# DRAINs on GpSimd's queue in the conditional blocks, and a tile's output products in one run with the next tile's score products

## The chip, the cores and the metric

One core of one Trainium2 chip runs the kernel. The metric is the device time of one execution in microseconds (us). Before the change three timed runs gave 1208.03, 1209.3 and 1210.64 us; their median, 1209.3 us, is what the change is measured against.

## What is computed

Three layers follow each other: attention inside chunks of 64 positions, a dense layer with three input matrices and a maximum between them, and a layer of eight experts of which each token takes one.

```python
scores = scale * np.matmul(q_c, k_c.transpose(0, 1, 2, 4, 3))     # 8 x 8 heads, chunks of 64 x 64
attn = softmax(scores); out = np.matmul(attn, v_c)
...
h = np.maximum(np.maximum(x @ w1, x @ w2), x @ w3)                # 4608 x 512 by 512 x 768
x = h @ w_out                                                     # 768 x 512
...
e_idx = np.argmax(x @ w_gate, axis=1)                             # one expert of 8 a token
h = np.maximum(x[mask] @ w1[e], 0.0)                              # 512 x 1024
ye = h @ w2[e]                                                    # 1024 x 512
out[mask] = gate_w[mask, None] * eom[mask, e, None] * ye
```

All is fp32; the wide products are made of three passes over split operands (`mm3`, lines 101 to 104).

## The kernel before

**Attention, 36 tiles.** A tile `a` is 128 positions of all eight heads. `att_S` (line 422) makes the scores: 16 products of 64 x 64, which TensorE does as quarters of its array, into the two banks of the PSUM tile `ps_a2` (the tiles 1 and 2 have other banks). VectorE takes the maxima (line 440), ScalarE the exponentials with their sums in eight ACTIVATEs (459), VectorE the reciprocals (465, 466), GpSimd the product with them (469). `att_P` (474) turns the result with four full transposes (485), and ScalarE copies it out (491). `att_V` (493) makes the outputs, again 16 quarter products (507), into `ps_a2` as well; ScalarE rounds them into `xth` (514) and VectorE makes the rest `xtl` (99). `quarters` (403) gives both the same first half of either bank: `[:, :, 0:HP * 64]`, that is 256 of 512 columns.

**Dense layer, nine blocks of four tiles.** `moe_f` (598) runs 18 groups of 12 matmuls of 128x512 per block (lines 102 to 104); ScalarE and VectorE bring them out over one buffer `hs` (611, 613), ScalarE and GpSimd split the result (615, 99). `moe_y` (618) and `gate` (637) follow.

**What sets the order.** In these two layers every step is recorded with an engine, an estimated duration, a priority and the keys that it reads and writes (`add`, 256); `order` (290) then plays the steps through and writes each engine's queue. So the order of each engine's instructions is fixed when the program is built, and TensorE has attention steps of the next block's tiles between the wide matmuls of the present block. A key that is read by two engines can be given an order of its own: line 271 does that for `psg` and for the tuples `("tr", ..)` and `("mm", ..)`. The key of `ps_a2` is the plain string `"a2"`, whose first character is `"a"`; the test `x[0] in ("a2", ..)` doesn't meet it.

`attention` (1051) calls the steps of a tile. From tile 7 (`2 * NA - 1`) to the last, the scores of tile `i + 1` are recorded after the outputs of tile `i` (the table `after`).

**Experts.** Tokens are gathered in blocks of 256 by expert. `step` (1149) does one block: GpSimd copies the places of block `b + 2` and gathers it (`gather_ahead`, 1133: a COPY and two indirect DMAs, lines 838 and 831), TensorE makes the two products, ScalarE scales the result (884), and GpSimd writes it with two indirect DMAs (887). 18 blocks (0 to 17) are written out straight; the rest, 18 to 25, are nested conditionals (`tail`, 1189), entered as long as the number of blocks is larger than `b`. This input has 21 blocks, so 18, 19 and 20 run. Code outside `order` runs in the order in which it is written. At the program's end each engine does a DRAIN, and a barrier follows; these and the preamble have the lines 1232 and 1212.

Of the kernel before, what the change touches and what calls it, by code (L numbers as in the profile page):

```python
# [21 lines left out]
def tile_chunk_attention_moe_moe(  # L22
# [25 lines left out]
    NTILE = NT // P  # L48
# [8 lines left out]
    NB0 = NT // BP  # L57
# [113 lines left out]
    HP = H // 2  # L171
# [88 lines left out]
    def add(eng, dur, prio, rd, wr, fn, lat=0.0, lead=0.0):  # L260
        o = Op()
        o.eng, o.dur, o.fn, o.prio, o.n = eng, dur, fn, prio, len(ops)
        o.lat, o.lead, o.at = lat, lead, None
        if eng == "PE" and lead == 0.0 and prio > 0:
            o.lead = LEAD
        need = set()
        rd, wr = list(flat(rd)), list(flat(wr))
        for x in rd:
            if x in writer:
                need.add(writer[x])  # L270
            if x == "psg" or x[0] in ("a2", "tr", "mm"):

                need.update(r for r in readers.get(x, ()) if r.eng != eng)
        for x in wr:
            if x in writer:
                need.add(writer[x])
            need.update(readers.get(x, ()))
        for x in rd:
            readers.setdefault(x, []).append(o)
        for x in wr:  # L280
            writer[x] = o
            readers[x] = []
        o.need, o.rd, o.wr = need, rd, wr
        ops.append(o)
# [115 lines left out]
        i = a % NE2  # L400
        return es[i], [("e", i), ("mx", i), ("sm", i)], mxs[i], sms[i]

    def quarters(a):


        sp = lambda x, n: x.rearrange("p (b x) -> p b x", b=n)[:, :, 0:HP * 64].rearrange("p b (a i) -> p b a i", a=HP)
        if a % 3 and a < NW:
            bk = [(ps_mm[0], ("mm", 0)), (ps_mm[1], ("mm", 1))] if a % 3 == 1 else [(ps_mm[2], ("mm", 2)), (ps_g, "psg")]
            return [(sp(x, 1), [kx], slice(i, i + 1)) for i, (x, kx) in enumerate(bk)]
        return [(sp(ps_a2, 2), ["a2"], slice(0, 2))]  # L410
# [7 lines left out]
    def att_Q(a, pr):  # L418
        for w in range(2):
            load(a, w, pr - LA)  # L420

    def att_S(a, pr):
        e, (ek, mk, sk), mx, sm = e_of(a)

        t = qk_buf[a % 3]
        parts = quarters(a)
        bank = [ps[:, i] for ps, _, hs in parts for i in range(hs.stop - hs.start)]

        def mm():
            for hp in range(HP):  # L430
                for h2 in range(2):
                    for c in range(2):
                        x = t[h64(h2), :, hp, h64(c)]
                        PE.matmul(bank[h2 if a < NAT else h2 ^ c][h64(c), hp], x[:, 0], x[:, 1], start=True, stop=True)

        add("PE", T_Q, pr + 1, [("qk", a % 3, 0), ("qk", a % 3, 1)], [x for _, kk, _ in parts for x in kk], mm)
        m2 = mx.rearrange("p (b a) -> p b a", b=2)
        for n, (ps, pk, hs) in enumerate(parts):
            add("DVE", t_dve(512 // len(parts)), pr + 1, pk, [(mk, n)],
                lambda ps=ps, hs=hs: DVE.tensor_reduce(out=m2[:, hs], in_=ps, axis=AX.X, op=ALU.max))  # L440
        ex = e.rearrange("p (a b) j -> p b a j", b=2)
        ek2, sk2 = [(ek, 0), (ek, 1)], [(sk, 0), (sk, 1)]
        if a in SUBD:
            for n, (ps, pk, hs) in enumerate(parts):
                add("DVE", t_dve(512 // len(parts)), pr + 1, pk + [(mk, n)], ek2 if len(parts) == 1 else [(ek, n)],
                    lambda ps=ps, hs=hs: DVE.tensor_tensor(
                        out=ex[:, hs], in0=ps, in1=m2[:, hs].unsqueeze(3).to_broadcast([P, hs.stop - hs.start, HP, 64]),
                        op=ALU.subtract))
            add("ACT", t_act(512), pr + 1, ek2, ek2, lambda: ACT.activation(out=e, in_=e, func=ACTF.Exp, scale=scale))
            add("DVE", t_dve(512), pr + 1, ek2, sk2, lambda: DVE.tensor_reduce(out=sm, in_=e, axis=AX.X, op=ALU.add))  # L450
        else:
            add("DVE", 0.08, pr + 1, [(mk, n) for n in range(len(parts))], [mk] + [(mk, n) for n in range(len(parts))],
                lambda: DVE.tensor_scalar(out=mx, in0=mx, scalar1=-scale, scalar2=None, op0=ALU.mult))  # L453
            for b in range(2):
                ps, pk, hs = parts[b % len(parts)]

                def fn(b=b):
                    for hp in range(HP):
                        ACT.activation(  # L459
                            out=ex[:, b, hp], in_=bank[b][:, hp], func=ACTF.Exp, scale=scale,  # L460
                            bias=mx[:, HP * b + hp:HP * b + hp + 1], accum_out=sm[:, 2 * hp + b:2 * hp + b + 1])

                add("ACT", 4 * 0.29, pr + 1, pk + [mk], [(ek, b), (sk, b)], fn)
        add("DVE", 0.08, pr + 1, sk2, sk2,
            lambda: DVE.tensor_scalar(out=sm, in0=sm, scalar1=1e-9, scalar2=None, op0=ALU.add))
        add("DVE", 0.12, pr + 1, sk2, sk2, lambda: DVE.reciprocal(out=sm, in_=sm))
        on = "DVE" if a < MULD else "POOL"
        add(on, t_dve(512) if on == "DVE" else 1.0, pr + 1, ek2 + sk2, ek2,
            lambda: (DVE if on == "DVE" else POOL).tensor_tensor(
                out=e, in0=e, in1=sm.unsqueeze(2).to_broadcast([P, H, 64]), op=ALU.mult))  # L470

    def att_P(a, pr):
        e, (ek, _, _), _, _ = e_of(a)
# [16 lines left out]
        add("PE", 0.9 if a < NAT else 0.45, pr + 2, [(ek, 0), (ek, 1)], [("tr", a % 2)], fn)  # L490
        add("ACT", t_act(512), pr + 2, [("tr", a % 2)], [("pTF", a % 2)], lambda: ACT.copy(pTF[a % 2], pp))

    def att_V(a, pr):
        j, t_ = tile_block[a]
        dst = lambda hl: xt[j % 2][hl][:, :, t_ * P:(t_ + 1) * P]
        xk = lambda hl: [("xt", j % 2, t_, hl, h2) for h2 in range(2)]
        vv, x = v_buf[a % NV], pTF[a % 2]
        bank = [ps[:, i] for ps, _, cs in quarters(a) for i in range(cs.stop - cs.start)]

        def mm():  # L500
            for hp in range(HP):
                for s in range(2):
                    for c in range(2):
                        if a < NAT:
                            PE.matmul(bank[c][h64(s), hp], vv[h64(c), hp, s], x[h64(c), hp, s], start=True, stop=True)
                        else:
                            PE.matmul(bank[c][h64(s ^ c), hp], vv[h64(s), hp, c], x[h64(s), hp, c], start=True, stop=True)

        add("PE", T_Q, pr + 3, [("v", a % NV), ("pTF", a % 2)], [x for _, kk, _ in quarters(a) for x in kk], mm)
        o = lambda hl: dst(hl).rearrange("p a (b i) -> p b a i", b=2)  # L510
        for ps, pk, cs in quarters(a):
            n = 256 * (cs.stop - cs.start)
            kx = lambda hl: [("xt", j % 2, t_, hl, i) for i in range(cs.start, 2)] if n == 256 else xk(hl)
            add("ACT", t_act(n), pr + 3, pk, kx(0), lambda ps=ps, cs=cs: ACT.copy(o(0)[:, cs], ps))
            add("DVE", t_dve(n), pr + 3, pk + kx(0), kx(1), lambda ps=ps, cs=cs: sub(DVE, o(1)[:, cs], ps, f(o(0)[:, cs])))
# [535 lines left out]
    def attention(a, n):  # L1051

        def prio(i):
            j, t = tile_block[i]
            return -100 + PS * i if j == 0 else A1 + AS1 * t if j == 1 else v0(j - 1) + AO + AS * t

        pr = [prio(i) for i in range(NTILE)]

        def score(i):
            if i < NTILE:  # L1060
                att_Q(i, pr[i])
                att_S(i, pr[i])


        before = {i: [i + 2] for i in (*range(NA - 2), NA, NA + 1)}
        after = {i: [i + 1] for i in range(2 * NA - 1, NTILE)}
        after[NA - 1] = [NA, NA + 1]
        if a == 0:
            score(0)
            score(1)  # L1070
        for i in range(a, a + n):
            att_P(i, pr[i])
            for x in before.get(i, ()):
                score(x)
            att_V(i, pr[i])
            for x in after.get(i, ()):
                score(x)

# [70 lines left out]
    def step(b):  # L1149
        scalars(b)  # L1150
        gather_ahead(b + 2)
        for c in range(4):
            for i in range(2):
                l1_mm(b, c, i)
            l1_hi(c)
            l1_lo(c)
            if c == 2:
                switch(b, (0,))
        x_T(b + 1)
        switch(b, (1,))  # L1160
        if b + 1 < NBLK:
            full[b + 1] = sval([ET.PE], 7, b + 1, 1)
        l2(b, 0)
        with tc.If(full[b] > 0):
            l2(b, 1)
        y(b, 1)
        switch(b, (2, 3))
# [69 lines left out]
```

## Time and profile before

| | |
|---|---|
| median of 3 timed runs | 1209.3 us |
| profiled execution | 1207.82 us |
| its span, first to last instruction | 1206.0 us |
| TensorE busy | 1181.2 us (98%), 9219 matmuls |
| VectorE, ScalarE, GpSimd busy | 436.7 (36%), 418.1 (35%), 195.7 (16%) us |
| TensorE's mean granted clock | 0.995 |

The profile is one execution. PE is TensorE with its matmuls, PEld its weight loads, DVE VectorE, ACT ScalarE, POOL GpSimd, SP SyncE; a q behind a name is the engine's queue (its sequencer), whose waits, branches and DRAINs aren't counted as busy. A matmul's row has its start and a modelled end, so distances between starts are what is read here. An idle time in brackets stands before the instruction, with what ended it.

### The profile page before, as it was taken

What the parts mean: (1) busy time and instruction counts of PE and PEld (TensorE: products, weight loads), DVE (VectorE), ACT (ScalarE), POOL (GpSimd) and SP (SyncE); (2) the same over time, 40 slices, a digit from 0 to 9 for tenths busy, and PEclk for the clock granted to TensorE, in tenths of its full rate; (3) what the DMA queues carried; (4) which work ended last, traced back from release to release, by engine and by line L of the source; (5) the groups of instructions that cost most, each with busy time, mean ns of one, the idle gap of its engine ahead of it and who ended that gap; (6) DMA issues with size and microseconds to landing.
All of it is one profiled execution on the core that took longest, in us unless ns stands there. A gap on an engine that the chain in (4) does not pass through costs nothing. (4 is left out here: it accounts for less than half of the span.)

```text
span 1206.0 us, 23510 instructions
## 1 busy us (share of the span) xinstructions
PE 1181.2 (98%) x9219; PEld 1035.3 (86%) x9219; DVE 436.7 (36%) x1095; ACT 418.1 (35%) x1192; POOL 195.7 (16%) x243
## 2 busy tenths in 40 slices
PE   7999999999999999999999999999999999999995
PEld 6879788897888988988879898989989989999994
DVE  7995413232232322322323452211266211511270
ACT  5575323333243332333322322212256212512271
POOL 1000111111211111111111112112112212112120
PEclk9999999999999999999999999999999999999998
DMA  8842212121121121211230015111156211511151
GB/s 283 245 140 71 86 30 87 47 58 59 35 80 53 47 69 36 80 54 35 73 106 36 1 45 201 54 45 53 46 207 241 100 44 48 180 45 62 38 171 29
DMA packets 84318, 103.06 MB, mean 85 GB/s; under 512 B 40287, under 2 KB 49503, under 8 KB 84192
## 3 DMA queue, kind: packets, MB, share of 16 engines
q1 hardware_dynamic: 77152, 79.82, 20.7%
q0 software_dynamic: 7040, 21.60, 5.6%
q8 instruction: 75, 1.23, 0.4%
q14 instruction: 51, 0.42, 0.1%
HBM read 149.55 MB, written 20.52 MB: 141 GB/s over the span
## 5 line engine op out<-in xcount | busy, mean ns | idle before, releaser
L102 PE MATMUL mm<-xth,wpc 128*128 128x512 f32 x576 | 233.8, 406 | 0.0
L104 PE MATMUL mm<-xth,wpc 128*128 128x512 f32 x576 | 226.5, 393 | 0.0
L103 PE MATMUL mm<-xtl,wpc 128*128 128x512 f32 x576 | 226.0, 392 | 0.1
L613 DVE TENSOR_TENSOR hs<-mm,hs 128x512 f32<-128x512 f32 x108 | 74.4, 688 | 184.0 <-PE mm L104 184.0
L871 DVE SCALAR_TENSOR_TENSOR wo<-mm,wo 128x512 fp32r<-128x512 f32 x64 | 43.5, 689 | 239.1 <-ACT wo L867 208.6
L104 PEld LDWEIGHTS mm<-xth,wpc 128*128 128x128 f32 x576 | 108.3, 188 | 24.7
L102 PEld LDWEIGHTS mm<-xth,wpc 128*128 128x128 f32 x576 | 108.2, 188 | 23.8
L103 PEld LDWEIGHTS mm<-xtl,wpc 128*128 128x128 f32 x576 | 108.5, 188 | 21.3 <-DVE xtl L99 0.4
L102 PE MATMUL mm<-wo,ht 128*128 128x256 f32 (+1 forms) x432 | 126.2, 292 | 0.0
L104 PE MATMUL mm<-wo,ht 128*128 128x256 f32 (+1 forms) x432 | 122.7, 284 | 0.0
L103 PE MATMUL mm<-wo,ht 128*128 128x256 f32 (+1 forms) x432 | 122.6, 284 | 0.0
L102 PE MATMUL tr<-wpc,wo 128*128 128x512 f32 x304 | 120.3, 396 | 0.0
L104 PE MATMUL tr<-wpc,wo 128*128 128x512 f32 x304 | 118.5, 390 | 0.0
L103 PE MATMUL tr<-wpc,wo 128*128 128x512 f32 x304 | 118.3, 389 | 0.0
L99 POOL TENSOR_TENSOR ht<-hs,ht 128x512 fp32r<-128x512 f32 x48 | 62.0, 1291 | 293.2 <-ACT ht L615 293.2
L887 POOL DMA_INDIRECT out_dram<-yo,S x42 | 43.7, 1042 | 355.2 <-ACT yo L884 271.4
L615 ACT CAST ht<-hs 128x512 fp32r<-128x512 f32 x54 | 33.6, 623 | 160.9 <-DVE hs L613 160.8
L459 ACT ACTIVATE rg<-a,mx 128x64 f32<-128x64 f32 x264 | 78.7, 324 | 22.1 <-DVE mx L453 22.1
L99 DVE TENSOR_TENSOR wpc<-raw,wpc 128x512 fp32r<-128x512 f32 x112 | 70.2, 684 | 39.8 <-ACT wpc L825 39.8
L102 PEld LDWEIGHTS mm<-wo,ht 128*128 128x128 f32 x432 | 81.2, 188 | 1.8 <-issue 0.4
L103 PEld LDWEIGHTS mm<-wo,ht 128*128 128x128 f32 x432 | 81.5, 189 | 0.4
L104 PEld LDWEIGHTS mm<-wo,ht 128*128 128x128 f32 x432 | 81.3, 188 | 0.0
(243 smaller groups left out, 2258.3 us busy)
## 6 DMA issues: line engine op xcount, KB each, us to landing
raw<-in_moe_w_dram SPq DMA_DIRECT2D x92, 1024.0 KB
x_scratch<-U SPq DMA_DIRECT2D x36, 258.0 KB
rg<-in_q_dram SPq DMA_DIRECT2D x36, 256.0 KB
rg<-in_k_dram SPq DMA_DIRECT2D x36, 256.0 KB
wst<-in_moe_w_dram SPq DMA_DIRECT2D x18, 512.0 KB
rg<-in_v_dram SPq DMA_DIRECT2D x128, 64.0 KB
U<-in_moe_w_out_dram SPq DMA_DIRECT2D x6, 512.0 KB
rg<-in_v_dram SPq DMA_DIRECT2D x4, 256.0 KB
```

Of the source, the lines that this page charges most:

```text
L99: eng.tensor_tensor(out=o, in0=a, in1=b, op=ALU.subtract)
L102: PE.matmul(o, ah, bh, start=first, stop=False)
L103: PE.matmul(o, ah, bl, start=False, stop=False)
L104: PE.matmul(o, al, bh, start=False, stop=last)
L459: ACT.activation(out=ex[:, b, hp], in_=bank[b][:, hp], func=ACTF.Exp, scale=scale, bias=mx[:, HP * b + hp:HP * b + hp + 1], accum_out=sm[: ...
L613: add("DVE", t_dve(N), up, [pk, hk], [hk], lambda: DVE.tensor_tensor(out=h, in0=ps, in1=h, op=ALU.max))
L615: add("ACT", t_act(N), up, [hk], [("ht", g, 0)], lambda: ACT.copy(ht[g][:, 0, :N], h))
L871: DVE.scalar_tensor_tensor(out=hT()[:, 1, fs], in0=l1_ps(c), scalar=0.0, in1=f(hT()[:, 0, fs]), op0=ALU.max, op1=ALU.subtract)
L887: POOL.indirect_dma_start(out=out, out_offset=bass.IndirectOffsetOnAxis(ap=ic[b % 4]()[:, t, 1:2].bitcast(U32), axis=0), in_=yo(b, t), in_ ...
```

## The change

Four things change. `quarters` gets a second parameter that chooses the half of the banks' columns. For the tiles 7 to 34 the outputs of tile `i` go to the second half and are recorded as one TensorE step with the scores of tile `i + 1`, which go to the first half; the step reads the keys of both, and `att_S` is a generator now that hands over its products and later records its VectorE, ScalarE and GpSimd steps behind the outputs' evictions. The key `"a2"` now gets the order between reading engines that line 271 names. And `step` issues a DRAIN on GpSimd behind `gather_ahead` in the conditional blocks.

```diff
-            if x == "psg" or x[0] in ("a2", "tr", "mm"):
+            if x in ("psg", "a2") or x[0] in ("tr", "mm"):
...
-    def quarters(a):
+    def quarters(a, h=0):
...
-        sp = lambda x, n: x.rearrange("p (b x) -> p b x", b=n)[:, :, 0:HP * 64].rearrange("p b (a i) -> p b a i", a=HP)
+        sp = lambda x, n: x.rearrange("p (b x) -> p b x", b=n)[:, :, h * HP * 64:(h + 1) * HP * 64].rearrange(
+            "p b (a i) -> p b a i", a=HP)
...
-    def att_S(a, pr):
+    def att_S(a, pr, alone=True):
...
-        add("PE", T_Q, pr + 1, [("qk", a % 3, 0), ("qk", a % 3, 1)], [x for _, kk, _ in parts for x in kk], mm)
+        if not alone:
+            yield mm
+        else:
+            add("PE", T_Q, pr + 1, [("qk", a % 3, 0), ("qk", a % 3, 1)], [x for _, kk, _ in parts for x in kk], mm)
...
+        yield
...
-    def att_V(a, pr):
+    def att_V(a, pr, score=None):
...
-        bank = [ps[:, i] for ps, _, cs in quarters(a) for i in range(cs.stop - cs.start)]
+        parts = quarters(a, 1 if score else 0)
+        bank = [ps[:, i] for ps, _, cs in parts for i in range(cs.stop - cs.start)]
+        with_it = next(score) if score else None
...
+            if with_it:
+                with_it()
+
+        qk = [("qk", (a + 1) % 3, w) for w in range(2)] if score else []
+        add("PE", 2 * T_Q - 0.3 if score else T_Q, pr + 3, [("v", a % NV), ("pTF", a % 2)] + qk,
+            [x for _, kk, _ in parts for x in kk], mm)
...
-        after = {i: [i + 1] for i in range(2 * NA - 1, NTILE)}
-        after[NA - 1] = [NA, NA + 1]
+        after = {NA - 1: [NA, NA + 1]}
...
-            att_V(i, pr[i])
+
+            s_ = None
+            if 2 * NA - 1 <= i < NTILE - 1:
+                att_Q(i + 1, pr[i + 1])
+                s_ = att_S(i + 1, pr[i + 1], False)
+            att_V(i, pr[i], s_)
+            if s_:
+                next(s_)
...
     def step(b):
         scalars(b)
         gather_ahead(b + 2)
+        if b >= NB0:
+            POOL.drain()
         for c in range(4):
```

**TensorE's queue, tiles 18 and 19, before.** First the outputs of tile 18 (L507), further down the scores of tile 19 (L434), its transposes (L485) and its outputs (L507). The L102 to L104 rows are wide matmuls; `x16` is a run of 16 quarter products, which the trace has as 32 matmuls. The numbers behind `rg` tell buffers apart (123 holds the exponentials, 124 their transposes, 121 and 122 q, k and v).

```order
L104 MATMUL mm_158<-xth_1109,wpc_144 128x512
L507 MATMUL a_155<-rg_124,rg_122 64x64 x16
L102 MATMUL mm_158<-xth_1109,wpc_144 128x512
...
L434 MATMUL a_155<-rg_121 64x64 x16
L102 MATMUL mm_156<-xth_1109,wpc_145 128x512
...
L485 MATMUL tr_154<-ident,rg_123 128x128 x4
L102 MATMUL mm_158<-xth_1109,wpc_145 128x512
L103 MATMUL mm_158<-xtl_1110,wpc_145 128x512
L104 MATMUL mm_158<-xth_1109,wpc_145 128x512
...
L507 MATMUL a_155<-rg_124,rg_122 64x64 x16
```

**The same place now.** L517 are outputs, L437 scores, L492 transposes.

```order
L104 MATMUL mm_157<-xth_1109,wpc_143 128x512
L517 MATMUL a_155<-rg_124,rg_122 64x64 x16
L437 MATMUL a_155<-rg_121 64x64 x16
L102 MATMUL mm_157<-xth_1109,wpc_143 128x512
...
L492 MATMUL tr_154<-ident,rg_123 128x128 x4
L102 MATMUL mm_156<-xth_1109,wpc_145 128x512
L103 MATMUL mm_156<-xtl_1110,wpc_145 128x512
L104 MATMUL mm_156<-xth_1109,wpc_145 128x512
...
L517 MATMUL a_155<-rg_124,rg_122 64x64 x16
L437 MATMUL a_155<-rg_122 64x64 x16
L102 MATMUL mm_156<-xth_1109,wpc_145 128x512
```

What moved: 39 wide matmuls stood between the outputs of tile 18 and the scores of tile 19, and none does now; from the scores to the transposes there were 27, and there are 54; from the transposes to the outputs six before and six now. The same pair stands in the queue 28 times, from outputs 7 with scores 8 to outputs 34 with scores 35.

**ScalarE's queue, the same two tiles, before.** L491 copies out the transposes (tile 18, then tile 19), L514 rounds the outputs, L459 are the eight exponentials of tile 19, L611 and L615 bring out the dense layer.

```order
L491 COPY rg_124<-tr_153 128x512
L514 CAST xth_131<-a_155 128x2x4x64
L615 CAST ht_137<-hs_141 128x512
L611 COPY hs_141<-mm_156 128x512
L615 CAST ht_138<-hs_141 128x512
L459 ACTIVATE rg_123,sm_129<-a_155,mx_126 128x64 x8
L611 COPY hs_141<-mm_156 128x512
L491 COPY rg_124<-tr_154 128x512
L514 CAST xth_131<-a_155 128x2x4x64
```

**And now**, with L498, L529, L465, L626 and L630 for the same steps.

```order
L498 COPY rg_124<-tr_153 128x512
L529 CAST xth_131<-a_155 128x2x4x64
L465 ACTIVATE rg_123,sm_129<-a_155,mx_126 128x64 x8
L630 CAST ht_137<-hs_141 128x512
L626 COPY hs_141<-mm_156 128x512
L498 COPY rg_124<-tr_154 128x512
L630 CAST ht_138<-hs_141 128x512
L529 CAST xth_131<-a_155 128x2x4x64
```

What moved: the exponentials of tile 19 stand right behind the rounding of tile 18's outputs, ahead of two casts and a copy of the dense layer that stood ahead of them. On VectorE likewise the maxima of tile 19 (L446) now stand right behind the `xtl` of tile 18 (L99).

## Rows read from the trace of the kernel before

**Rows 1.** The page's first part: engine, busy us, share of the span, instructions.

```profile
PE 1181.2 (98%) x9219; PEld 1035.3 (86%) x9219; DVE 436.7 (36%) x1095; ACT 418.1 (35%) x1192; POOL 195.7 (16%) x243
```

**Rows 2.** Busy time by stretch: start:end, us, per engine, PE's granted clock.

```profile
300.00:400.00 100.00, 100.00 (x808) 83.44 (x801) 28.41 (x82) 32.85 (x123) 17.27 (x18) 1.00 0.19 54
1180.00:1206.00 26.00, 11.78 (x56) 9.53 (x54) 2.08 (x3) 3.15 (x5) 2.02 (x2) 0.78 0.04 13
```

**Rows 3.** Timeline of PE: start us, us, instruction, count; scores, transposes and outputs of tile 19.

```profile
308.71 0.39 PE L103 MATMUL mm<-xtl,wpc 128*128 128x512 f32 x1
308.95 0.40 PE L104 MATMUL mm<-xth,wpc 128*128 128x512 f32 x1
309.27 0.69 PE L434 MATMUL a<-rg 64*64 64x64 f32 x32
309.90 0.50 PE L102 MATMUL mm<-xth,wpc 128*128 128x512 f32 x1
310.24 0.39 PE L103 MATMUL mm<-xtl,wpc 128*128 128x512 f32 x1
...
316.27 0.60 PE L485 MATMUL tr<-ident,rg 128*128 128x128 f32 x4
...
318.18 0.69 PE L507 MATMUL a<-rg,rg 64*64 64x64 f32 x32
318.81 0.50 PE L102 MATMUL mm<-xth,wpc 128*128 128x512 f32 x1
```

**Rows 4.** Timeline of PE at the start: quarter runs that follow each other.

```profile
17.14 0.69 PE L505 MATMUL mm<-rg,rg 64*64 64x64 f32 x32
17.66 0.65 PE L434 MATMUL a<-rg 64*64 64x64 f32 x32
18.12 0.22 PE L482 MATMUL tr<-ident,rg 64*64 64x64 f32 x1
```

**Rows 5.** Timeline of PE, scores of tile 8 and the instruction before them.

```profile
81.23 0.66 PE L571 MATMUL psg<-ident,rg 128*128 128x128 f32 x4
82.84 0.69 PE L434 MATMUL a<-rg 64*64 64x64 f32 x32 [0.95 <-DVE xtl L99]
```

**Rows 6.** Timeline of ACT, tile 19: first and last exponential, copy out.

```profile
311.03 0.31 ACT L459 ACTIVATE rg<-a,mx 128x64 f32<-128x64 f32 x1 [0.30 <-DVE mx L453]
...
313.35 0.62 ACT L611 COPY hs<-mm 128x512 f32<-128x512 f32 x1
```

**Rows 7.** Lines 1232, 1192 and 1212 by queue: ns min/median/max, first and last start us.

```profile
L1232 POOLq DRAIN  x3: 46/107/7261, 1197.9 to 1205.7; - x3
L1232 SPq DRAIN  x3: 7/7/13, 1198.4 to 1205.4; - x3
L1192 POOLq INC_SWDGE_SEM  x1: 1960/1960/1960, 1195.8 to 1195.8; - x1
L1212 POOLq INC_SWDGE_SEM  x1: 31/31/31, 0.2 to 0.2; - x1
L1212 POOLq DRAIN  x1: 184/184/184, 0.4 to 0.4; - x1
```

**Rows 8.** Lines 831 and 887: the indirect DMAs of POOL, and time to landing.

```profile
L831 POOL DMA_INDIRECT xg<-x_scratch,S x46: 942/993/1466, 704.7 to 1176.0; - x46
DMA to landing us min/median/max: 3.2/3.7/6.4
L887 POOL DMA_INDIRECT out_dram<-yo,S x42: 997/1015/1442, 740.5 to 1192.8; - x42
```

**Rows 9.** Timeline of POOL, blocks 18 to 20: the write behind each pair of gathers.

```profile
1150.59 1.02 POOL L887 DMA_INDIRECT out_dram<-yo,S  x1 [13.85 <-ACT yo L884]
...
1169.03 1.01 POOL L887 DMA_INDIRECT out_dram<-yo,S  x1 [9.06 <-ACT yo L884]
...
1187.34 1.01 POOL L887 DMA_INDIRECT out_dram<-yo,S  x1 [10.40 <-ACT yo L884]
1192.78 1.00 POOL L887 DMA_INDIRECT out_dram<-yo,S  x1 [4.42 <-ACTq L1120]
```

More of the change, by code (lines that the diff above doesn't have):

```diff
@@ L507, in mm @@
                             PE.matmul(bank[c][h64(s ^ c), hp], vv[h64(s), hp, c], x[h64(s), hp, c], start=True, stop=True)
-        add("PE", T_Q, pr + 3, [("v", a % NV), ("pTF", a % 2)], [x for _, kk, _ in quarters(a) for x in kk], mm)
+            if with_it:
[3 more added lines that the diff above has]
+            [x for _, kk, _ in parts for x in kk], mm)
         o = lambda hl: dst(hl).rearrange("p a (b i) -> p b a i", b=2)
-        for ps, pk, cs in quarters(a):
+        for ps, pk, cs in parts:
             n = 256 * (cs.stop - cs.start)
@@ L1059, in score @@
         def score(i):
-            if i < NTILE:
-                att_Q(i, pr[i])
-                att_S(i, pr[i])
+            att_Q(i, pr[i])
+            next(att_S(i, pr[i]))
         before = {i: [i + 2] for i in (*range(NA - 2), NA, NA + 1)}
-        after = {i: [i + 1] for i in range(2 * NA - 1, NTILE)}
-        after[NA - 1] = [NA, NA + 1]
+        after = {NA - 1: [NA, NA + 1]}
         if a == 0:
```

## Prediction

> **What bounds the kernel now.** First the page's busy times, then busy time by stretch, then TensorE's timeline, and last the queues at the end. TensorE is busy for 1181.2 of 1206.0 us [rows 1]; in the attention and dense stage it has no idle time at all, while VectorE and ScalarE are busy for about 30 of 100 us [rows 2]. So what TensorE does there counts at its full length, and what the others do counts only where TensorE comes to wait. A busy PE is not PE at its best, though: the distances between starts show what a run of quarter products really takes. The other place is the end. In the last 26 us TensorE is busy for 11.8 [rows 2], GpSimd issues its last write at 1192.78 [rows 9], and behind it stand two queue instructions of GpSimd alone, an INC_SWDGE_SEM of 1.96 us and a DRAIN of 7.26 us [rows 7], the end of which is almost the end of the program. These two are the path there.
>
> **The merged runs.** A wide matmul starts 0.24 us after the one before (308.71 and 308.95). With the scores of tile 19 between them, two wide starts lie at 308.95 and 309.90, and the next, also late, at 310.24 [rows 3]. From 308.95 to 310.24 are 1.29 us for two pitches of 0.23 and one run: the run costs 0.83 us, in three parts: 0.63 from its first start to the next wide one, 0.09 that its start is late, 0.11 that the second wide matmul is late. The outputs' run takes the same 0.63 (318.18 to 318.81) [rows 3]. What a run costs directly behind another of its kind the start of the kernel shows: 17.14, 17.66, 18.12 [rows 4], so 0.46 us for one that has a quarter run before and behind it, and 0.52 for the one that begins the sequence. So entering and leaving quarter work is about 0.37 of the 0.83 us, and a merged pair pays it once. The order of TensorE's queue has 28 such pairs now. Saved: 28 x (0.83 - 0.46) = **10.3 us**. The bounds are 28 x (0.83 - 0.52) = 8.7 us, and 28 x 0.83 = 23 us if the second run went entirely into the first one's shadow, which 17.66 to 18.12 speaks against; I take 10.3.
>
> One of the 28 has a wait besides: the scores of tile 8 stood idle for 0.95 us until VectorE had read the outputs of tile 7 out of the same banks [rows 5]. In one run nothing is read between the two, so the wait goes: **0.95 us**, or nothing if VectorE, busy there with weights, makes another step late.
>
> What the merging moves: scores come 39 wide matmuls earlier, and 54 instead of 27 stand between them and their transposes. Before, that distance was 316.27 - 309.27 = 7.0 us and no wait shows at the transposes [rows 3]; now it is about twice that. The outputs stand six wide matmuls behind the transposes in either order. The new "a2" order adds one wait that bites: the exponentials on ScalarE stand right behind the rounding of the outputs, and between them VectorE must do the rest and the maxima. Queued behind the waiting exponentials are a cast and a copy of the dense layer, which empty the banks of the wide matmuls. The eight exponentials take 2.32 us (311.03 to 313.35) [rows 6]; with the rounding, two VectorE steps and their signals, ScalarE is out of reach for some 5 us after a merged run. TensorE comes back to a bank after two groups of 12 matmuls, 24 x 0.23 = 5.6 us after it has filled it. That covers it, narrowly at worst, so I put the wait at zero. The bounds are 0 and 0.5 us for a tile, 0 to 14 us in all; zero is the nearer end, since at the neighbouring tiles the same exponentials stood ahead of such a copy [rows 6] without a stall.
>
> **The DRAINs.** GpSimd's DRAINs in this trace last 0.046, 0.107 and 7.26 us at the end and 0.184 us in the preamble; the two short ones at the end follow the long one [rows 7]. INC_SWDGE_SEM lasts 0.031 us at the start and 1.96 us at the end [rows 7]. So neither has a fixed price; something that has piled up by then is worked off, and a DRAIN leaves little behind. What GpSimd has issued by then is 46 + 42 = 88 indirect DMAs [rows 8]; 7.26 us over 88 is 0.083 us for each. I take it that this is what piles up. Three of the new DRAINs are executed, in the blocks 18, 19 and 20. The first finds 78 DMAs (88 less ten from there on), 6.4 us of work, the other two four each, 0.3 us. They must have the gathers landed first, which takes 3.7 us from issue [rows 8], 2.7 from the end of the instruction. All three lie in a stretch in which GpSimd has nothing to do until the block's first output is ready, 13.85, 9.06 and 10.40 us [rows 9]. The first needs 2.7 + 6.4 = 9.1 of its 13.85 us; so they cost **0**. Should each last 7.26 us, the second would overrun its 9.06 us by 0.9, and the write that it delays has no reader in the program.
>
> At the end two DMAs are left, so the DRAIN falls from 7.26 to some 0.2 us. What is late next is SyncE, whose own DRAIN there began at 1198.4 [rows 7], against the end of GpSimd's at 1197.9 + 7.26 = 1205.2. The gain is 1205.2 - 1198.5 = **6.7 us**. The INC_SWDGE_SEM, if it falls in the same proportion, to below 0.1 us, gives **1.9 us** more, since SyncE comes to its last waits behind it. The bounds of the two are 0 (they stay as long) and 8.6 us.
>
> Here a page speaks against the change. The Trainium skill, VectorE: DVE Perf Modes, section "The DRAIN you can't avoid", says that the DRAINs around a kernel are about 12 ns each, constant, on all five engines. The trace agrees for SyncE (7 to 13 ns) and not for GpSimd (46 to 7261 ns) [rows 7]. By that rule a DRAIN in a block could take nothing off the last one, and the sum would lose its last two terms, which is the first rival.
>
> **Sum.** 10.3 + 0.95 + 6.7 + 1.9 = 19.9 us off the profiled execution's 1207.8 us gives 1187.9. The three timed runs had a median 1.5 us above that execution; on their scale it is 1209.3 - 19.9 = **1189.4 us**.
>
> **Rivals.**
> (1) *The last DRAIN stays*, because its 7.26 us don't come from the DMAs since the last DRAIN but from the program's end. For it: no DRAIN inside the kernel is in this trace, and 88 is only one way to divide. Against it: the short ones, all on the same queue. Then 11.25 us are saved: 1198.0 us.
> (2) *The merged run pays twice*, because outputs and scores read other buffers and write the other half of the same banks, and TensorE settles between them as before. For it: [rows 4] is a run into other banks. Against it: 32 products of one run already go through both banks without a stop. Then the gain is 0.95 + 8.6 = 9.55: 1199.7 us.
> (3) *ScalarE becomes the bound of the stage*, and the kernel is slower. Its place is the copy of `hs` behind the exponentials, its price the time by which ScalarE's roughly 5 us exceed the 5.6 us that a bank can wait. It decides the sign from 19.9 / 28 = 0.71 us for each tile, that is from 6.3 us out of reach; with 1 us the kernel takes 1189.4 + 28 = 1217 us, with 0.2 us 1195. For it: the exponentials wait for two VectorE steps where they waited for one. Against it: ScalarE is idle for two thirds of the stage [rows 2].
> (4) *Nothing arrives*: the new DRAINs hold GpSimd until TensorE waits for its gather, and this eats what the runs save. Against it: 9 to 14 us of cover [rows 9], and a gather is two blocks ahead. About 1208 us.
>
> **How the numbers follow.** The forecast, 1186 to 1192 us with the bounds of its terms, has 0.70; rival 1 0.14, rival 2 0.06, rival 3 0.07 (0.04 with a small wait, 1192 to 1200 us, and 0.03 slower than before), rival 4 0.03. To leave out no more than 2 in 10 the range reaches to rival 1: 1185 to 1199.5 us. About 0.2% (2.4 us) is what a measurement of this kernel can tell from no change. Faster by more than that: 0.70 + 0.14 + 0.06 + 0.04 + 0.01 = 0.95; within it 0.02; slower 0.03.
>
> **What would show it.** Right is: the 28 score runs start about 0.5 us behind an output run, with one late wide matmul behind each pair; PE's list of waits has no new entry at the wide matmuls (rival 3 would be one behind an `hs` copy); in the blocks 18 to 20 GpSimd's queue has DRAINs, the first some 6 to 9 us long and the others short; the last one is below 0.5 us, and SyncE's is the last to end. If the DRAINs in the blocks are all near 7 us, or all near 0.1 us with the last at 7, rival 1 holds and my account of 88 DMAs is wrong. If the second run of a pair takes 0.6 us or more, rival 2 does.

## The result, and the profile after

The changed kernel takes 1190.9 us (median of four runs, 1190.3 to 1191.4) against 1209.4 (four runs, 1208.0 to 1210.6): a ratio of 0.985, with a 95% interval of 0.983 to 0.986. That is 18.5 us less; the prediction had 19.9 us, 1189.4 us, and a range of 1185.0 to 1199.5. The profiled execution took 1190.56 us. Its page begins, to be held against [rows 1]:

```profile
span 1188.8 us, 23369 instructions
PE 1172.4 (99%) x9219; PEld 1035.3 (87%) x9219; DVE 432.5 (36%) x1095; ACT 416.3 (35%) x1192; POOL 194.4 (16%) x243
```

TensorE has as many instructions as before and is busy for 8.8 us less. The outputs of tile 19, which stood apart from any scores [rows 3], now stand in one run with the scores of tile 20. The timeline of TensorE there (start us, us, engine, line, operation, count; L517 are the outputs, L437 the scores, L102 to L104 the wide matmuls):

```profile
308.63 0.40 PE L104 MATMUL mm<-xth,wpc 128*128 128x512 f32 x1
308.96 0.69 PE L517 MATMUL a<-rg,rg 64*64 64x64 f32 x32
309.47 0.65 PE L437 MATMUL a<-rg 64*64 64x64 f32 x32
310.05 0.50 PE L102 MATMUL mm<-xth,wpc 128*128 128x512 f32 x1
310.39 0.39 PE L103 MATMUL mm<-xtl,wpc 128*128 128x512 f32 x1
```

From 308.63 to 310.39 are 1.76 us; less two pitches of 0.23, the pair costs 1.30 us. Before, its two runs cost 2 x 0.83 = 1.66 us by [rows 3]. The saving is 0.36 us for this pair.

The sum over all pairs is best read as the time between two matmuls that every kernel has. All 28 pairs lie between the 208th and the last of the 1944 wide matmuls that read the attention's result. The starts of these two in the traces are:

| kernel | 208th, us | last, us | between |
|---|---|---|---|
| before | 88.74 | 700.74 | 612.00 |
| after | 89.94 | 692.12 | 602.18 |

So the merged runs brought 9.8 us, 0.35 for each pair. What lies ahead of the 208th differs from execution to execution, and not with the change: the first wide matmul starts at 31.34 us in the trace of before, at 31.84 and 32.60 in two more without the merged runs, and between 31.06 and 32.92 in four traces of kernels that have the change's merged runs and differ only in their DRAINs. The changed kernel's profiled execution was 0.9 us late there, so the profiled pair differs by 17.3 us and the medians by 18.5.

At the end, the queues of GpSimd and SyncE (ns min/median/max, first and last start us), to be held against [rows 7]:

```profile
L1173 POOLq DRAIN  x3: 5354/6643/8411, 1126.1 to 1166.1; - x3
L1254 POOLq DRAIN  x3: 46/107/212, 1187.4 to 1188.5; - x3
L1254 SPq DRAIN  x3: 7/7/13, 1187.9 to 1188.2; - x3
L1214 POOLq INC_SWDGE_SEM  x1: 231/231/231, 1186.9 to 1186.9; - x1
```

L1173 are the new DRAINs. The last DRAIN fell from 7.26 to 0.21 us, the INC_SWDGE_SEM from 1.96 to 0.23. From the start of the last write (1184.05) to the end of the span (1188.8) are 4.75 us, where [rows 9] and the span of [rows 1] give 1206.0 - 1192.78 = 13.2. The end brought 8.5 us, and from the last of the wide matmuls in the table to that write both have the same, 492.0 and 491.9 us. 9.8 and 8.5 are 18.3 of the 18.5 us.

The timeline of GpSimd shows the second gather of the blocks 18, 19 and 20 (L846), beside which a DRAIN now stands, and the write behind it (L902). The idle time ahead of the writes, in brackets, is that of [rows 9]:

```profile
1127.05 0.97 POOL L846 DMA_INDIRECT xg<-x_scratch,S  x1 [0.30 <-issue]
1141.87 1.02 POOL L902 DMA_INDIRECT out_dram<-yo,S  x1 [13.85 <-ACT yo L899]
...
1150.28 0.98 POOL L846 DMA_INDIRECT xg<-x_scratch,S  x1 [0.30 <-issue]
1160.31 1.02 POOL L902 DMA_INDIRECT out_dram<-yo,S  x1 [9.05 <-ACT yo L899]
...
1167.25 0.97 POOL L846 DMA_INDIRECT xg<-x_scratch,S  x1 [0.30 <-issue]
1178.61 1.02 POOL L902 DMA_INDIRECT out_dram<-yo,S  x1 [10.39 <-ACT yo L899]
```

### The profile page after: what moved, and what is told of

Same layout as the page of the kernel before. It is cut to its first block, busy times and chain, and to the rows that moved or that the text cites. A ratio compares the mean times of both kernels' runs of the same rounds, so it can differ in the third digit from the quotient of the medians.

```text
span 1188.8 us, 23369 instructions
## 1 busy us (share of the span) xinstructions
PE 1172.4 (99%) x9219; PEld 1035.3 (87%) x9219; DVE 432.5 (36%) x1095; ACT 416.3 (35%) x1192; POOL 194.4 (16%) x243
## 5 line engine op out<-in xcount | busy, mean ns | idle before, releaser
L102 PE MATMUL mm<-xth,wpc 128*128 128x512 f32 x576 | 231.4, 402 | 0.0
L104 PE MATMUL mm<-xth,wpc 128*128 128x512 f32 x576 | 226.3, 393 | 0.0
L104 PEld LDWEIGHTS mm<-xth,wpc 128*128 128x128 f32 x576 | 108.4, 188 | 24.5
L102 PEld LDWEIGHTS mm<-xth,wpc 128*128 128x128 f32 x576 | 108.2, 188 | 23.5
L102 PE MATMUL mm<-wo,ht 128*128 128x256 f32 (+1 forms) x432 | 125.6, 291 | 0.0
L104 PE MATMUL mm<-wo,ht 128*128 128x256 f32 (+1 forms) x432 | 122.7, 284 | 0.0
L102 PE MATMUL tr<-wpc,wo 128*128 128x512 f32 x304 | 120.2, 396 | 0.0
L104 PE MATMUL tr<-wpc,wo 128*128 128x512 f32 x304 | 118.5, 390 | 0.0
L902 POOL DMA_INDIRECT out_dram<-yo,S x42 | 43.9, 1044 | 352.7 <-ACT yo L899 268.6
L99 POOL TENSOR_TENSOR ht<-hs,ht 128x512 fp32r<-128x512 f32 x48 | 61.9, 1290 | 192.3 <-ACT ht L630 192.3
L465 ACT ACTIVATE rg<-a,mx 128x64 f32<-128x64 f32 x264 | 79.3, 326 | 34.5 <-DVE mx L459 34.4
L99 DVE TENSOR_TENSOR wpc<-raw,wpc 128x512 fp32r<-128x512 f32 x112 | 70.3, 685 | 39.8 <-ACT wpc L840 39.8
L102 PEld LDWEIGHTS mm<-wo,ht 128*128 128x128 f32 x432 | 81.3, 188 | 1.3 <-issue 0.4
L882 ACT ACTIVATE wo<-mm 128x512 fp32r<-128x512 f32 x64 | 38.2, 598 | 124.8 <-PE mm L104 119.3
L104 PEld LDWEIGHTS mm<-wo,ht 128*128 128x128 f32 x432 | 81.3, 188 | 0.0
```

What stands on the lines that cost most here:

```text
L99: eng.tensor_tensor(out=o, in0=a, in1=b, op=ALU.subtract)
L102: PE.matmul(o, ah, bh, start=first, stop=False)
L104: PE.matmul(o, al, bh, start=False, stop=last)
L465: ACT.activation(out=ex[:, b, hp], in_=bank[b][:, hp], func=ACTF.Exp, scale=scale, bias=mx[:, HP * b + hp:HP * b + hp + 1], accum_out=sm[: ...
L882: ACT.activation(out=hT()[:, 0, 2 * c:2 * c + 2], in_=l1_ps(c), func=ACTF.Relu)
L902: POOL.indirect_dma_start(out=out, out_offset=bass.IndirectOffsetOnAxis(ap=ic[b % 4]()[:, t, 1:2].bitcast(U32), axis=0), in_=yo(b, t), in_ ...
```

## The experiments

### Each part alone

Only the DRAINs, on the kernel before:

```diff
         gather_ahead(b + 2)
+        if b >= NB0:
+            POOL.drain()
```

> The kernel before with only the DRAINs in the blocks; the quarter runs stay apart. Theory (GpSimd's DRAIN works off the indirect DMAs issued since its last one): the three DRAINs in the blocks last 5 to 8.5 us, the last one about 0.2 us, INC_SWDGE_SEM about 0.23 us as in the changed kernel, and the end comes about 8.5 us earlier: 1209.4 - 8.5 = 1200.9 us. First rival of the prediction (the last DRAIN has its length from the program's end, and falls for another reason in the changed kernel): the last DRAIN stays near 7.3 us and the time at 1209.4. A second rival, that the DRAINs hold GpSimd and the gain of the changed kernel at the end is partly eaten before it: between 1201 and 1209, with TensorE idle at a gather.

Measured: 1200.2 us, ratio 0.9932 (0.9916 to 0.9949), 8.3 us less than the kernel before measured beside it (1208.5). Its queue rows:

```profile
L1153 POOLq DRAIN  x3: 5621/7516/8417, 1135.5 to 1175.6; - x3
L1234 POOLq DRAIN  x3: 46/107/212, 1196.7 to 1197.8; - x3
L1194 POOLq INC_SWDGE_SEM  x1: 231/231/231, 1196.3 to 1196.3; - x1
```

The time between the two wide matmuls stays at 612.00 us. The whole gain lies at the end, and both rivals fall.

Only the merged runs, that is the changed kernel without these two lines:

> The changed kernel without the DRAINs in the blocks: only the merged runs and the new order of the outputs' banks. Theory: the two parts add up, the milestones of TensorE fall back by about 10 us between 118 and 643 us, the last DRAIN is back at about 7.3 us and INC_SWDGE_SEM at about 1.96: 1209.4 - 10.1 = about 1199.4 us. If the merged runs bring the end more than that (because the DRAIN's cost depends on what stands around it), the time is below 1198 and the drains-only kernel gains less than 8 us.

Measured: 1199.1 us, ratio 0.9926 (0.9908 to 0.9945), 9.4 us less than before. Between the two wide matmuls are 602.14 us, the last DRAIN lasts 7.26 us again and the INC_SWDGE_SEM 1.96. 8.3 + 9.4 = 17.7 us, within the intervals of 18.5: the parts add up.

Only the new order at the outputs' banks:

```diff
-            if x == "psg" or x[0] in ("a2", "tr", "mm"):
+            if x in ("psg", "a2") or x[0] in ("tr", "mm"):
```

> The kernel before with only the new rule for the outputs' banks (every reader of another engine is waited for), which moves ScalarE's and VectorE's steps at the outputs and no product of TensorE. Theory: no effect of its own, 1209.4 us, and the first wide matmul at 31.3 us as before. Rival (the changed kernel reached its first wide matmul 0.9 us and block 118 us 1.4 us later than the kernel before because of this rule): 1210.3 to 1210.8 us, with the first wide matmul at 32.2.

Measured: 1208.5 us, ratio 0.9994 (0.9984 to 1.0003), and 612.07 us between the two wide matmuls: no effect of its own. The first wide matmul starts at 31.84 us in its trace, about half way between the two expected numbers, so that start decides nothing; the time does.

### What a pair saves

One dummy product over the whole array between outputs and scores, into a bank of the transposes:

```diff
             if with_it:
+                warm(ps_tr[a % 2])
                 with_it()
```

and, as the control, in a kernel of its own, the same product behind both:

```diff
             if with_it:
                 with_it()
+                warm(ps_tr[a % 2])
```

In both, the step is also recorded as a writer of that bank.

> The changed kernel with one dummy matmul over the whole array (128x128, bf16, into a transposition bank) between the outputs and the scores of each merged pair. Theory (the gain is that a pair enters and leaves quarter work once): the pair pays twice again, 28 x (0.37 + 0.06) = 12 us more than the changed kernel's 1190.9, so about 1202.8 us, and the scores' run starts some 0.9 us behind the outputs' run. Rival (the gain comes from something else, such as the wide matmuls that no longer wait for scores or the other order of the banks): only the dummy itself is paid, 28 x 0.056 = 1.6 us, so about 1192.5 us.

> The control to the run with a dummy matmul between: the same dummy matmul behind each merged pair, where whole-array work begins anyway. Theory (entering and leaving is what costs): only the dummy itself is paid, 28 x 0.056 = 1.6 us on the changed kernel's 1190.9, about 1192.5 us. If a dummy costs as much here as between the runs, its price is its own (its weights, its bank) and the comparison says nothing on entering and leaving.

Measured: 1198.4 us with the dummy between (0.9921, 0.9905 to 0.9938), 1191.5 with it behind (0.9859, 0.9843 to 0.9876). Between the two wide matmuls are 610.92 and 602.70 us, so a pair costs (610.92 - 602.18) / 28 = 0.31 us more in the first and 0.02 in the control. The timeline of TensorE, dummy (L288) between:

```profile
311.58 0.69 PE L517 MATMUL a<-rg,rg 64*64 64x64 f32 x32
312.21 0.23 PE L288 MATMUL tr<-ones_b 128*128 128x128 bf16 x1
312.37 0.69 PE L437 MATMUL a<-rg 64*64 64x64 f32 x32
313.00 0.50 PE L102 MATMUL mm<-xth,wpc 128*128 128x512 f32 x1
```

and behind:

```profile
310.11 0.69 PE L517 MATMUL a<-rg,rg 64*64 64x64 f32 x32
310.63 0.65 PE L437 MATMUL a<-rg 64*64 64x64 f32 x32
311.21 0.23 PE L288 MATMUL tr<-ones_b 128*128 128x128 bf16 x1
311.25 0.48 PE L102 MATMUL mm<-xth,wpc 128*128 128x512 f32 x1
```

With a product over the whole array behind it, the first run takes 0.63 us to the next start instead of 0.52; the dummy takes 0.16, and the second run 0.63 instead of 0.58. That is 0.11 + 0.16 + 0.05 = 0.32. The control shows that the dummy as such is nearly free. So it is entering and leaving quarter work that costs here, and the rival falls: both kernels keep the new order and the other half of the banks, and only the one with the dummy between the runs loses most of the gain. One crossing there and back is 0.31 us with the dummy in it. The Trainium skill, TensorEngine Tiling (Array Packing), section "Key Properties", says that a change of the tiling mode drains TensorE; the traces agree in that a crossing costs time, 0.63 us to the next start instead of 0.52. But the theory had 12 us and the traces give 8.7 (the medians 7.5). Missing was 0.11 us for each pair, the late second whole-array product of [rows 3]. The next run, with three dummies, asks whether a single one is too few to show it:

> As the run with one dummy matmul between the runs of a pair, but with three. There a pair cost 0.31 us more than in the changed kernel, not 0.43. Theory (a product over the whole array behind a quarter run delays the whole-array product after it by some 0.1 us, which a single dummy never pays, since the next one is a quarter again): the second dummy starts about 0.16 us behind the first, the third 0.06 behind the second, and a pair costs 0.31 + 0.06 + 0.06 + 0.1 = 0.53 us more than in the changed kernel, 28 x 0.53 = 15 us on 1190.9, about 1205.7 us. Rival (entering and leaving is the 0.31 us and there is no late second product here): the dummies lie 0.06 us apart, 28 x 0.43 = 12 us, about 1202.9 us.

Measured: 1203.4 us (0.9945, 0.9929 to 0.9962), and 614.13 us between the two wide matmuls: (614.13 - 602.18) / 28 = 0.43 us for a pair, the rival's number. The three dummies of one pair:

```profile
315.74 0.69 PE L517 MATMUL a<-rg,rg 64*64 64x64 f32 x32
316.37 0.34 PE L288 MATMUL tr<-ones_b 128*128 128x128 bf16 x3
316.64 0.69 PE L437 MATMUL a<-rg 64*64 64x64 f32 x32
317.26 0.50 PE L102 MATMUL mm<-xth,wpc 128*128 128x512 f32 x1
317.60 0.40 PE L103 MATMUL mm<-xtl,wpc 128*128 128x512 f32 x1
```

From the first dummy to the scores are 0.27 us instead of 0.16, so two more dummies cost 0.06 each and the second is not late. The second wide matmul is late again: 0.34 us instead of 0.23. The 0.11 us thus came with the wide matmuls, not with these small products. Nor is it peculiar to quarter work: in the changed kernel the second wide matmul behind whole-array transposes of 128 columns is late as well, 0.32 us behind the first (85.95 and 86.27, shown with the 29th pair below), and 0.31 or 0.32 behind all 21 such runs that wide matmuls follow after 85 us; behind the twelve products of 256 to 288 columns it is 0.23 or 0.24. Why (size, type, the load of the weights) wasn't tried. Of the 0.36 us that a pair saves, 0.25 (0.31 less the dummy's 0.06) is shown to be the crossing; the other 0.11 is read from the rows alone, and goes with the interruption of the wide matmuls by narrow products, of which a merged pair makes one instead of two.

### What a DRAIN of GpSimd works off

One DRAIN alone, in block 18 (`NB0`), and in a second kernel in block 10 (`b == 10`):

```diff
-        if b >= NB0:
+        if b == NB0:
             POOL.drain()
```

> The changed kernel with one DRAIN alone, in block 18. Theory (about 0.08 us for each indirect DMA since the last DRAIN): the one in the block stays at about 8.4 us, ten DMAs are left at the end instead of two, and the last DRAIN lasts 0.212 + 8 x 0.082 = 0.87 us. Rival (a DRAIN's length has to do with its place, or one DRAIN anywhere makes the last one short): 0.21 us as with three.

> The changed kernel with one DRAIN alone, in block 10, where 46 indirect DMAs have been issued and 42 come after it. Theory (0.08 us for each since the last DRAIN): the one in the block works for about 46 x 0.08 = 3.7 us behind the landing of the last gather, and the last one lasts 42 x 0.082 = 3.5 us; the time is about 3.3 us above the changed kernel's. Rival (only what is issued late counts, or only scatters, or only gathers): the last one stays at 7.3, or falls to 0.2 us.

Measured: 1189.7 and 1192.8 us, one run each. Queue rows of the first and of the second kernel:

```profile
L1173 POOLq DRAIN  x1: 8411/8411/8411, 1124.8 to 1124.8; - x1
L1254 POOLq DRAIN  x3: 46/107/874, 1186.2 to 1187.6; - x3
L1214 POOLq INC_SWDGE_SEM  x1: 400/400/400, 1185.6 to 1185.6; - x1
```

```profile
L1173 POOLq DRAIN  x1: 6517/6517/6517, 943.0 to 943.0; - x1
L1254 POOLq DRAIN  x3: 52/107/3492, 1186.7 to 1190.8; - x3
L1214 POOLq INC_SWDGE_SEM  x1: 1040/1040/1040, 1185.5 to 1185.5; - x1
```

| indirect DMAs since the last DRAIN | last DRAIN, us | INC_SWDGE_SEM, us |
|---|---|---|
| 2 (three DRAINs) | 0.212 | 0.231 |
| 10 (one, block 18) | 0.874 | 0.400 |
| 42 (one, block 10) | 3.492 | 1.040 |
| 88 (none) | 7.261 | 1.960 |

Both numbers are straight lines: 0.082 us for each DMA in the DRAIN, and 0.020 in the INC_SWDGE_SEM on top of some 0.19. The expected 0.87 and 3.5 us arrived. The rivals (its place, one DRAIN anywhere, one kind of DMA only) fall. The four points hold 0, 4, 20 and 46 gathers and 2, 6, 22 and 42 writes, and one line fits them all, so a gather and a write cost about the same; whether a DMA counts as one or by its bytes stays open.

Two numbers expected of block 10 didn't arrive. Its DRAIN ends at 949.5 us, 4.5 us behind the end of its second gather (at 945.0), where 2.7 us for the landing, as in the prediction, and 3.7 make 6.4; the landing of that gather isn't in the trace. And the time is 1.9 us above the changed kernel's, not 3.3; that is one run against a median. In the traces, the program ends 500.4 us behind the last wide matmul of the table above, against 496.6 in the changed kernel.

### The 29th pair

The outputs of tile 4 and the scores of tile 7 in one run too (the scores of tile 7 are taken out of the table of those recorded ahead):

```diff
-            if 2 * NA - 1 <= i < NTILE - 1:
...
+            nx = 7 if i == 4 else i + 1 if 2 * NA - 1 <= i < NTILE - 1 else None
+            if nx:
...
```

> The changed kernel with the 29th pair merged as well: the outputs of tile 4 and the scores of tile 7, where the wait of 0.99 us for VectorE stands that the prediction had wrongly counted among the 28. Theory: the wait and one entering and leaving go, 1190.9 - (0.37 + 0.99) = 1189.5 us. Rival (there VectorE is busy with weights, so the same time is waited for at a later step): 1190.9 us, with another wait of TensorE of about 1 us behind it.

Measured: 1191.4 us (0.9849, 0.9835 to 0.9862), as without it. There the changed kernel still has the wait of [rows 5]:

```profile
81.75 0.69 PE L517 MATMUL a<-rg,rg 64*64 64x64 f32 x32
82.38 0.66 PE L586 MATMUL psg<-ident,rg 128*128 128x128 f32 x4
84.02 0.69 PE L437 MATMUL a<-rg 64*64 64x64 f32 x32 [0.99 <-DVE xtl L99]
...
85.56 0.64 PE L492 MATMUL tr<-ident,rg 128*128 128x128 f32 x4
85.95 0.48 PE L102 MATMUL mm<-xth,wpcr 128*128 128x512 f32 x1
86.27 0.39 PE L103 MATMUL mm<-xtl,wpcr 128*128 128x512 f32 x1
```

With the 29th pair merged it is gone, and two others stand in its place:

```profile
81.36 0.69 PE L517 MATMUL a<-rg,rg 64*64 64x64 f32 x32
81.88 0.65 PE L437 MATMUL a<-rg 64*64 64x64 f32 x32
82.45 0.66 PE L586 MATMUL psg<-ident,rg 128*128 128x128 f32 x4
83.59 0.66 PE L492 MATMUL tr<-ident,rg 128*128 128x128 f32 x4 [0.49 <-DVE rg L475]
84.08 0.98 PE L594 MATMUL psg<-gwr,U 128*128 128x16 f32 x8
85.46 0.50 PE L102 MATMUL mm<-xth,wpcr 128*128 128x512 f32 x1 [0.40 <-DVE hs L628]
```

From the outputs to the next wide matmul are 4.20 us in the one and 4.10 in the other. VectorE is busy without a gap there (3.00 of 3.00 us in the windows below), so TensorE waits for its next step instead: the rival.

## Why the prediction was right, and where not

**The merged runs, 10.3 us expected, 9.8 measured.** The mechanism held: one crossing into quarter work and back for a pair. The pair shown above costs 1.30 us, where the prediction had 0.83 + 0.46 = 1.29 by [rows 3, 4]; over all 28 the mean saving is 0.35 us instead of 0.37. The sum took one price for all. In the trace, 19 of the pairs stand between wide matmuls and cost 1.29 or 1.30 us; for the nine that stand beside other products [rows 3] gives no price, and the 9.8 us leave them 0.33 us each. Rival 2, that a pair pays twice, would have left the 612 us as they were. The prediction's own sign of it, a second run of 0.6 us or more, was a poor one: the second run takes 0.58, because the way back to whole-array work is in it. With a dummy between the runs it takes 0.63.

**The wait of 0.95 us, expected to go, stayed.** This step was wrong. The prediction took the scores in [rows 5] for those of tile 8 behind the outputs of tile 7. They are tile 7's, behind the outputs of tile 4, the first tile whose outputs come from line 507; that is not one of the 28 pairs. It had been read from the stretch of time and not from the order of the tiles. And the term was false a second way: merging that pair too gains nothing, since VectorE is the bound there. The prediction had named that end too (0.95 us or nothing), and had put the better one into its sum.

**ScalarE, expected 0.** Right. Between 90 and 690 us TensorE has no wait at all in its list, in the changed kernel as in the one before, and the new order alone changes nothing (ratio 0.9994). Rival 3 falls. The estimate of some 5 us holds as well. ScalarE at the outputs of tile 18 and the scores of tile 19:

```profile
294.54 0.59 ACT L529 CAST xth<-a 128x512 fp32r<-128x512 f32 x1 [1.81 <-PE a L437]
297.16 0.31 ACT L465 ACTIVATE rg<-a,mx 128x64 f32<-128x64 f32 x1 [2.03 <-DVE mx L459]
...
299.61 0.62 ACT L630 CAST ht<-hs 128x512 fp32r<-128x512 f32 x1
302.66 0.59 ACT L626 COPY hs<-mm 128x512 f32<-128x512 f32 x1 [2.43 <-POOL ht L99]
```

From the rounding to the end of the exponentials are 5.1 us (294.54 to 299.61), with 2.03 us of waiting in them. The next copy that empties a bank of the wide matmuls starts only at 302.66, after another 2.43 us in which ScalarE waits for GpSimd: it isn't the exponentials that hold it. In seven of the 28 pairs a copy stands between the rounding and the exponentials besides.

**The DRAINs in the blocks, expected to cost 0.** Right in the cost: the writes stand where they stood, with 13.85, 9.05 and 10.39 us of idle time. The account of their lengths was half right. The first starts at 1126.1 us, lasts 8.4 and ends 6.5 us behind the end of the second gather, which is what 78 DMAs take by the table (78 x 0.082 = 6.4); the landing of the gather does not come on top, as the prediction had added it: in the kernel with the DRAINs alone, whose trace has it, that gather landed 4.0 us after its start at 1136.5, some 3.5 us before the DRAIN ended at 1144.0. The others were called short and are recorded with 6.64 and 5.35 us. Their records begin before the second gather has run, and they end 4.7 and 3.2 us behind it, with little to work off. What they last for is the landing of that gather: in block 19 it landed 5.4 us after its start at 1150.28, at 1155.7, and the DRAIN ended at 1155.9. Six of the kernels' traces have such a landing for block 19 or 20, ten in all, and each time the DRAIN ended 0.21 us behind it. By the prediction's own test "all near 7 us" would have spoken for rival 1; the last DRAIN at 0.21 us decides against it. Rival 4 falls too: TensorE's only wait for a gather, at 701.2 us, is 0.70 us long, and was 0.74 before.

**The end, 8.6 us expected, 8.5 measured.** The division of 7.26 us by 88 DMAs was the right one, and rival 1 falls with the four points of the table. As foreseen, SyncE's DRAIN (1187.9) is now later than the end of GpSimd's (1187.6). The page that spoke against the change, VectorE: DVE Perf Modes in the Trainium skill, section "The DRAIN you can't avoid", with its about 12 ns on all engines, does not hold for GpSimd here, whose DRAINs at the end are 0.046 to 7.26 us [rows 7]; for SyncE (7 to 13 ns) it does. The INC_SWDGE_SEM was taken to fall in proportion, below 0.1 us; it fell to 0.23, because it has a part of 0.19 us that does not go. That is 0.15 us.

The three misses, 0.95 + 0.5 + 0.15, are 1.6 us; the forecast was 1.5 us too low.

## What to carry to other kernels

Quarter products pay for each border with whole-array ones: here 0.36 of the 0.83 us of a run went when it joined another. Count the borders, and put neighbouring runs together where their banks allow it. Where a queue's closing instructions are on the path, look at what they work off, and have it done earlier under an idle stretch of that engine. And before a wait goes into a sum, find out by tile, not by time, which instruction it belongs to, and whether the engine that is waited for is free behind it.

## What the runs showed of the hardware

GpSimd's DRAIN took 0.082 us for each indirect DMA issued since its last DRAIN, and INC_SWDGE_SEM 0.020 us for each on top of 0.19, over 2 to 88 DMAs. With four left to work off, the DRAIN ended 0.21 us behind the landing of the gather issued just before it.

Three of the traces, of the kernel with the 29th pair, of the one with the new order alone and of the one with three dummies, show TensorE at a lower clock for some microseconds behind its idle times near 83 us (a mean of 0.66 from 85 to 90 us in each). The windows of the kernel with the 29th pair (us; busy time and count for PE, PEld, DVE, ACT, POOL; granted clock; DMA share; GB/s):

```profile
82.00:85.00 3.00, 2.51 (x52) 2.17 (x44) 3.00 (x8) 2.40 (x5) 0.00 (x0) 1.00 0.70 242
85.00:90.00 5.00, 4.60 (x14) 3.56 (x14) 5.00 (x12) 2.48 (x4) 0.00 (x0) 0.66 0.74 212
```

and of the changed kernel:

```profile
82.00:85.00 3.00, 2.01 (x71) 1.64 (x62) 3.00 (x9) 2.21 (x4) 0.00 (x0) 1.00 0.58 181
85.00:90.00 5.00, 5.00 (x31) 4.31 (x31) 5.00 (x12) 3.55 (x6) 0.00 (x0) 1.00 0.73 198
```

Such a mean is a part of the stretch at the lower level of 1.2 GHz; wide matmuls then start 0.43 us apart instead of 0.23. Seven such pitches follow each other in the kernel with the 29th pair, 1.4 us more than at the full clock. The changed kernel had an idle time of 0.99 us there and kept the full clock, so what decides it stays open. In the kernel with the new order alone the lower clock was the largest part of the 2.5 us by which its profiled execution reached the 208th wide matmul later than before.
